# Attention and a gated convolution on one core: value products as half-row blocks between score couples

## The chip, the cores and the metric

The kernel runs on one core of one Trainium2 chip. The time is the device time of one launch in microseconds. Five runs of the kernel before gave 386.9, 384.28, 387.31, 382.95 and 384.23 us, a median of 384.28 us. The first of them is the one that was profiled: 386.9 us, of which the profile's span covers 385.1 us.

## The reference: what is computed

Eight batches, twelve heads, 448 positions, 64 numbers a head. First attention with a softmax that has an extra one in its sum; then, on the heads laid side by side (448 x 768), a projection to three parts, a circular convolution of the second part along the sequence by Fourier transform, the product of the three, and a last projection.

```
scores = (q @ k^T) / sqrt(64);  m = max over keys
attn   = exp(scores - m) / (sum exp(scores - m) + exp(-m) + 1e-9)
x      = heads of (attn @ v) side by side            # 8 x 448 x 768
x1, x2, x3 = split(x @ w_proj)                       # 768 -> 3 * 768
conv   = irfft(rfft(x2) * rfft(filter))              # along the 448 positions
out    = (x1 * conv * x3) @ w_out
```

The kernel leaves the maximum out, since exp(s - m) / (sum exp(s - m) + exp(-m)) is exp(s) / (sum exp(s) + 1).

## The kernel before

**Attention** works on pairs of heads, 48 of them (six a batch). The heads of a pair lie in the two halves of the 128 rows (64 numbers each). The 448 keys of a head are three tiles of 128 and a remainder of 64; the two remainders of a pair share one tile. So a pair has:

- a *score couple* for each of three key tiles (L770): two matmuls of 64 rows, one on each half of the array's rows, 448 columns each, into two adjacent PSUM banks; ACT takes the exponential of both at once (L777, 128 x 896 out of PSUM);
- one score matmul of the shared remainder tile (L772, all 128 rows) and its exponential (L783);
- the *rests* (L795): eight matmuls of 64 rows, alternating between the two halves, that multiply the remainder's exponentials with its values and start the sums of the value products;
- the *value products* (L803): 24 matmuls of all 128 rows and 65 columns (64 values and a column of ones, which gives the softmax sum); 12 for each head, into a bank for each head;
- `norm` on DVE (L816 to L818): one added, reciprocal, product, out of PSUM into `xb`; for some pairs a transpose on TensorE follows (L897), for the others a DMA transpose.

**The dense part** of a batch follows its attention: projection of the second part on folded data (L977), spectrum (L1004), product with the filter's spectrum on DVE, inverse (L1089), gates (L1050), last projection (L1162). It is worked on while the next batches' attention runs. The filter's own spectrum (L722, L725) is made once at the start, from `uw` (L715 on DVE), which waits for the DMA of the filter (L664) on POOL's queue.

**The order of all work** is made on the host before the program is written. Every step is a task with an engine, a cost, a wanted time (`ATT`, `SLOT`, `DENSE`, `PACE`, `FOLD`, `LOAD` and so on are the numbers that make the wanted times), what it needs and makes, and which buffers it takes and gives back. `Plan.run` walks through time and starts, on each engine, the first task in order of wanted time that is ready by the planner's account; the instructions are then written in that order. Each engine runs its own list strictly in that order. The eight PSUM banks are handed out by the planner (`spots`): score couples ("sc") and a pair's output ("op") take two adjacent banks, at most two of each at a time (`CAP`), everything else ("hy") one bank. `fillers` puts matmuls on an idle tile (L1248) into gaps of TensorE that the planner sees between 3 and 36 us of its clock.

Before the change, two score couples are usually one task (`both`), often with the previous pair's rests in the same task; the two heads' value products are a task each (`out_rest`).

Of the kernel before, what the change touches and what calls it, by code (L numbers as in the profile page):

```python
# [18 lines left out]
B, H, S, DH = 8, 12, 448, 64  # L19
D = H * DH  # L20
SP = 112
NST = S // SP
# [19 lines left out]
class Plan:  # L42
# [17 lines left out]
    FILL = (3.0, 36.0, 0.6)  # L60
    PAIRS = ("sc", "op")
    CAP = {"sc": 2, "op": 2, "hy": 5}
# [6 lines left out]
    def add(self, eng, cost, want, emit, need=(), make=(), take=(), give=(), dma=0.0, run=256, n=1, after=0.0, begun=(), late=0.0):  # L69
        self.tasks.append((want, len(self.tasks), eng, cost, emit, need, make, take, give, dma, after, run, n, begun, late))  # L70

    def run(self):
# [109 lines left out]

        while any(queue.values()):
            moved = False
            for e in queue:
                if free[e] > now + 1e-9:
                    continue
                for i, t in enumerate(queue[e][: self.WINDOW]):
                    if ready(t):
                        break  # L190
                else:
                    continue
                del queue[e][i]
# [10 lines left out]
                end = free[e] = now + t[3]  # L204
# [52 lines left out]
def kernel(  # L257
# [16 lines left out]
    EARLY1 = 3.56  # L274
    ATT = [0.74, 31.12, 90.92, 107.97, 154.61, 193.46, 231.91, 282.14]
    SLOT = [2.70, 6.66, 5.08, 5.83, 4.70, 0.35, 4.90, 4.50]
    DENSE = [45.16, 85.16, 124.09, 170.16, 216.54, 256.31, 315.08, 409.78]
    PACE = [2.27, 2.24, 1.74, 2.16, 1.15, 2.13, 0.54, 0.88]
    FOLD = [-0.15, 0.76, -31.49, -25.60, 10.65, 0.32, 9.43, 0.88]
    BPS = 1.26  # L280
    RE1 = 16.91
    WT = 2.03
    FT = 18.78
    HALVED = (2,)
    AHEAD = [0, 0, 46.94, 46.01, 34, 34, 34, 34]
    LEAD = [-8.41, 6.91, 5.34, 23.10]
    LOADS = ((1, 0), (1, 1), ("F", None), (0, None), (2, None), ("O", None))
    LOAD = [36.34, 20.13, 13.48, 39.00, 39.88, 46.37]
    STEP = 4.27
    FOLD0 = (39.83, 49.48, 37.97)  # L290
# [464 lines left out]

    T = {}

    def attention(i):
# [41 lines left out]
        def out_rest(u):  # L800
            for n in range(NST):
                for t in range(3):
                    nc.tensor.matmul(  # L803
                        out_bank(u)[:, n, :],
                        P["e"][1 + t][:, u * S + n * 128 : u * S + n * 128 + 128],
                        vn[b % 2][:, hp, 4 * u + t, :],
                        start=False,
                        stop=(n == NST - 1 and t == 2),
                    )
# [522 lines left out]
```

## Time and profile before

| | |
|---|---|
| median of five runs | 384.28 us (382.95 to 387.31) |
| the profiled run, and its span | 386.9 us, 385.1 us |
| TensorE matmuls | 3732, busy 369.9 us (96% of the span) |
| ACT, DVE, POOL busy | 265.7, 257.8, 113.4 us |
| TensorE busy in the first 40 us | 33.11 us |
| mean granted TensorE clock | 0.996 |
| moved by DMA | 58.73 MB, most of it in the first 125 us |

A group's line in the profile names the line of the kernel, the engine, the operation, what it writes and reads, the shape (rows\*columns of the weights, then the output) and how many there are; then the time that the engine was busy with them. A matmul's duration is its way through the array (some 190 ns for 65 columns); in a row of matmuls the next one starts long before, so the cost of one in a row is the distance between starts. In the timeline a line is a run of equal instructions: start, time to the end of the last one, and in brackets the idle time ahead of it and what ended it.

### The profile page before, as it was taken

The numbers are of one execution on the slowest core, as the hardware profiler recorded it, in microseconds if no ns is written. First come the engines' busy times: TensorE is split into PE (matmuls) and PEld (weight loads), VectorE is DVE, ScalarE is ACT, GpSimd is POOL, SyncE is SP. The second block draws the span as 40 slices with busy tenths as digits, with TensorE's granted clock in tenths as the row PEclk, the third lists the DMA queues.
The fourth block names the chain that finished last, engine by engine and source line by source line (L and its number), as shares of the span: only waits on it lengthen the run. The fifth ranks groups of instructions, "written<-read, shape, count | busy, mean of one in ns | idle before, by whom it ended". The sixth has DMA issues, their size and how long they took to land.

```text
span 385.1 us, 9634 instructions
## 1 busy us (share of the span) xinstructions
PE 369.9 (96%) x3732; PEld 236.6 (61%) x3732; DVE 257.8 (67%) x679; ACT 265.7 (69%) x460; POOL 113.4 (29%) x232
## 2 busy tenths in 40 slices
PE   8986999999999999999998999999999999999995
PEld 7655775566655666655764566556665567557653
DVE  6575849954888448975399748592489635971870
ACT  5876878555877869777776767678677776543543
POOL 5674934341761633543544421100000000000000
PEclk9998999999999999999999999999999999999999
DMA  9999999999999999999999943912220042103004
GB/s 208 257 216 249 220 226 206 136 171 203 221 208 183 195 278 208 214 192 258 242 239 150 232 116 92 213 43 103 62 31 2 2 124 69 43 0 124 0 2 163
DMA packets 134573, 58.73 MB, mean 153 GB/s; under 512 B 99389, under 2 KB 130944, under 8 KB 134528
## 3 DMA queue, kind: packets, MB, share of 16 engines
q1 hardware_dynamic: 97104, 48.35, 56.9%
q0 software_dynamic: 37184, 9.54, 27.5%
q8 instruction: 29, 0.48, 0.6%
q10 hardware_dynamic: 240, 0.23, 0.3%
q14 instruction: 16, 0.13, 0.1%
HBM read 43.86 MB, written 11.01 MB: 142 GB/s over the span
## 4 chain that ended last, share of the span: by engine, by line
PE 64%; DVE 17%; DMA 11%; issue 2%; POOL 2%; SPq 2%; ACT 1%; DVEq 0%; POOLq 0%
PE psum L1050 16%; PE psum L977 13%; PE psum L1162 13%; PE psum L803 7%; PE psum L770 6%; DVE t L1018 3%; DMA nat<-in_v_dram 3%; DMA filt<-in_moe_filter_fft_dram 3%; DMA kT<-nat 2%; DVE g L1065 2%; DMA nat<-in_q_dram 2%; DVE yh L1024 2%; PE psum L1004 2%; DVE xf L954 2%; PE psum L772 2%
## 5 line engine op out<-in xcount | busy, mean ns | idle before, releaser
L777 ACT ACTIVATE e<-psum 128x896 bf16<-128x896 f32 x144 | 125.6, 923 | 23.7 <-PE psum L770 23.1
L1050 PE MATMUL psum<-xT,wproj_bf 128*128 128x448 bf16 x576 | 121.2, 352 | 0.6 <-DVE g L1065 0.5
L1050 PEld LDWEIGHTS <-wproj_bf 128*128 128x128 bf16 x576 | 54.0, 97 | 44.8 <-issue 2.2
L977 PE MATMUL psum<-wproj_bf,xf 128*113 128x384 bf16 x384 | 69.6, 327 | 0.0
L977 PEld LDWEIGHTS <-xf 128*113 128x113 bf16 x384 | 49.4, 132 | 13.4 <-issue 1.9
L1162 PE MATMUL psum<-wout_bf,yT 128*128 128x384 bf16 x288 | 51.9, 326 | 0.2 <-DVE yT L1133 0.2
L1062 ACT CAST x<-psum 128x448 bf16<-128x448 f32 x48 | 25.7, 534 | 34.2 <-PE psum L1050 32.5
L803 PE MATMUL psum<-vn,e 128*128 128x65 bf16 x1152 | 45.2, 195 | 0.0
L1065 DVE TENSOR_TENSOR g<-x,psum 128x448 bf16<-128x448 bf16 x48 | 29.6, 616 | 19.4 <-PE psum L1050 18.1
L599 POOL CAST vn<-nat 128x192 bf16<-128x192 f32 x72 | 26.8, 399 | 51.9 <-DMA nat<-in_v_dram 38.0
L770 PE MATMUL psum<-qT,kT 64*128 64x448 bf16 x288 | 41.5, 358 | 0.0
L803 PEld LDWEIGHTS <-e 128*128 128x128 bf16 x1152 | 39.6, 98 | 2.8
L1174 ACT COPY osb<-psum 128x384 f32<-128x384 f32 x56 | 26.3, 485 | 20.3 <-PE psum L1162 19.8
L1162 PEld LDWEIGHTS <-yT 128*128 128x128 bf16 x288 | 27.3, 98 | 19.3 <-issue 1.6
L816 DVE TENSOR_SCALAR rec<-psum 128x8 f32<-128x8 f32 x48 | 7.8, 163 | 43.5 <-PE psum L803 42.7
L1018 DVE TENSOR_TENSOR t<-xs,hrs 113x768 bf16<-113x768 bf16 (+1 forms) x64 | 34.8, 581 | 2.5 <-ACT xs L1012 2.4
L818 DVE TENSOR_TENSOR xb<-psum,rec 128x512 bf16<-128x512 f32 x48 | 33.2, 691 | 1.7
L533 POOL DMA_DIRECT2D nat<-in_q_dram x28 | 24.9, 890 | 31.8 <-DMA qT<-nat 15.6
L989 DVE CAST x<-psum 113x384 bf16<-113x384 f32 x32 | 17.7, 553 | 24.4 <-PE psum L977 23.9
L1012 ACT CAST xs<-psum 113x384 bf16<-113x384 f32 (+1 forms) x64 | 28.0, 493 | 4.1 <-PE psum L1004 4.0
L991 ACT CAST x<-psum 113x384 bf16<-113x384 f32 x32 | 15.4, 481 | 19.7 <-PE psum L977 19.4
L1098 ACT CAST cr<-psum 128x452 bf16<-128x452 f32 x48 | 25.4, 551 | 5.0 <-PE psum L1089 4.8
(109 smaller groups left out, 447.5 us busy)
## 6 DMA issues: line engine op xcount, KB each, us to landing
nat<-in_k_dram SPq DMA_DIRECT2D x48, 192.0 KB, 5.2
nat<-in_v_dram SPq DMA_DIRECT2D x48, 192.0 KB, 5.3
out_dram<-osb SPq DMA_DIRECT2D x24, 384.0 KB, 2.7
nat<-in_q_dram POOLq DMA_DIRECT2D x20, 168.0 KB, 7.0
nat<-in_q_dram SPq DMA_DIRECT2D x11, 224.0 KB, 7.3
wproj_bf<-in_moe_w_proj_dram POOLq DMA_DIRECT2D x2, 1152.0 KB, 18.3
rests<-in_k_dram SPq DMA_DIRECT2D x8, 192.0 KB, 5.9
rests<-in_v_dram SPq DMA_DIRECT2D x8, 192.0 KB, 6.8
```

The costliest lines, as they stand in the source:

```text
L599: nc.gpsimd.tensor_copy(vn[b % 2][:, hp, 4 * u : 4 * u + 3, 0:DH], sv[:, u])
L770: nc.tensor.matmul(sc[:, u, 0:S], kT[b % 2][c, hp, t, :], qT[b % 2][c, hp, :])
L777: nc.scalar.activation(e[:, 0 : 2 * S].rearrange("p (u n) -> p u n", u=2), pair(("sc", ("S", i, t)))[:, :, 0:S], AF.Exp, scale=SCALE,)
L803: nc.tensor.matmul(out_bank(u)[:, n, :], P["e"][1 + t][:, u * S + n * 128 : u * S + n * 128 + 128], vn[b % 2][:, hp, 4 * u + t, :], start= ...
L818: nc.vector.tensor_tensor(W["xb", b][:, hp].rearrange("p n (u d) -> p u n d", u=2), op[:, :, :, 0:DH], rec[:].unsqueeze(3).to_broadcast([1 ...
L977: nc.tensor.matmul(pps[:FQ, :DCH], W["xf", b][:, pg, kt, 0:FQ], wproj_bf[:, kt, D + ch * DCH : D + (ch + 1) * DCH], start=(kt == 0), stop= ...
L1012: nc.scalar.copy(L["xs", par, ch][:K, pg % 2, :], L["Z", pg, ch][:K, :DCH])
L1018: nc.vector.tensor_tensor(t[:K], L["xs", par, ch][:K], h, op=ALU.mult)
L1050: nc.tensor.matmul(p[:, :S], wproj_bf[:, kt, 2 * part * D + dt * 128 : 2 * part * D + (dt + 1) * 128], xT()[:, kt, 0:S], start=(kt == 0), ...
L1065: nc.vector.tensor_tensor(g[:, dt, :], L["x1", dt], p[:, :S], op=ALU.mult)
L1162: nc.tensor.matmul(ops[:n, :DCH], y[:, dt, 0:n], wout_bf[:, dt, ch * DCH : (ch + 1) * DCH], start=(dt == 0), stop=(dt == NDT - 1),)
L1174: nc.scalar.copy(L["os", st][:n, ch * DCH : (ch + 1) * DCH], L["O", st, ch][:n, :DCH])
```

## The change

1. Every value product of 128 rows is split into two of 64 rows, one on each half of the array, so that the pair's products are 48 matmuls in place of 24. They come in two blocks of 24 (`values(0)`, `values(1)`): in the first, the lower half adds into head 0's bank and the upper half into head 1's; in the second the halves are swapped, so that the two matmuls that run beside each other never write the same bank. The second block's first matmul waits by a semaphore (`half_done`) until the first block's last one has written.
2. Score couples are single tasks; the rests and the first block are one task (`way`), the second block another. By their wanted times they follow each other as: couple 1 of pair i, rests and first block of pair i-1, couple 2, second block, couple 3.
3. Up to three score pairs may hold banks (`CAP`), in place of two.
4. The planner books a cost for each change on TensorE between tasks of half-row matmuls (`row`) and others (`TURN`); it lets TensorE wait up to `WAIT` for the next half-row task when it has just done one; it avoids putting a second block directly behind its first one (`apart`, `REACH`, `CLOSE`).
5. All wanted times are new numbers, so that the order of everything is new.

```diff
-    CAP = {"sc": 2, "op": 2, "hy": 5}
+    REACH = 2.43
+    TURN = 0.1
+    CLOSE = 0.12
+    WAIT = 0.31
+    CAP = {"sc": 3, "op": 2, "hy": 5}
...
-                    if ready(t):
+                    if near is not None and t[0] > queue[e][near][0] + self.REACH:
                         break
-                else:
+                    if not ready(t):
+                        if e == "PE" and t[15] and prev and prev[15]:
+                            later = soon(t)
+                            if later <= now + self.WAIT:
+                                heapq.heappush(events, max(later, now + 1e-6))
+                                hold = True
+                                break
+                        continue
+                    if prev is not None and t[16] in prev[6]:
+                        near = i if near is None else near
+                        continue
+                    at = i
+                    break
...
+                end = now + t[3]
+                if e == "PE":
+                    if close:
+                        end += self.CLOSE
+                    if t[15] != bool(prev and prev[15]):
+                        end += self.TURN
+                    prev = t
...
-    ATT = [0.74, 31.12, 90.92, 107.97, 154.61, 193.46, 231.91, 282.14]
+    ATT = [0.36, 42.32, 102.52, 113.36, 162.99, 193.84, 245.07, 281.01]
...
-        def out_rest(u):
+        def values(side):
+
             for n in range(NST):
                 for t in range(3):
-                    nc.tensor.matmul(
-                        out_bank(u)[:, n, :],
-                        P["e"][1 + t][:, u * S + n * 128 : u * S + n * 128 + 128],
-                        vn[b % 2][:, hp, 4 * u + t, :],
-                        start=False,
-                        stop=(n == NST - 1 and t == 2),
-                    )
+                    for low in range(2):
+                        u = low ^ side
+                        c = slice(64 * low, 64 * low + 64)
+                        now = nc.tensor.matmul(
+                            out_bank(u)[:, n, :],
+                            P["e"][1 + t][c, u * S + n * 128 : u * S + n * 128 + 128],
+                            vn[b % 2][c, hp, 4 * u + t, :],
+                            start=False, stop=(side == 1 and n == NST - 1 and t == 2),
+                        )
+                        if side and not n + t + low:
+                            behind(now, P["V"])
+            if not side:
+                P["V"] = mark(now)
...
+            if t:
+                add("PE", 0.195, tau(i) + 0.002 * t if i else w, lambda t=t: scores(t),
+                    need=[("kT", i), ("qT", i)] + ([("S", i, t - 1)] if t > 1 else [("S", i - 1, 3)] if i else []),
+                    make=[("S", i, t)], take=[("sc", ("S", i, t))], row=True)
...
+        def way():
+            out_rests()
+            values(0)
+
+        add("PE", 0.53, w + 0.003, way, need=[("e", i), ("ones", b % 2), "pads", ("v", i), ("vr", b)], make=[("V", i)],
+            take=[("op", i)], give=[("er", (i, 0))], row=True)
+        add("PE", 0.395, w + 0.005, lambda: values(1), need=[("V", i)], make=[("V", i, 0), ("V", i, 1)],
+            give=[("e", (i, t)) for t in range(1, 4)], row=True, apart=("V", i))
```

`mark` lets the matmul that it is given add one to `half_done`; `behind` lets a matmul wait until `half_done` has reached a count. `soon` gives the planner's time at which a half-row task that is not ready yet will be.

## The prediction

> **What bounds the kernel now.** I read the page's busy times first, then its slices and the chain of work that ended last.
>
> ```profile
> PE 369.9 (96%) x3732; PEld 236.6 (61%) x3732; DVE 257.8 (67%) x679; ACT 265.7 (69%) x460; POOL 113.4 (29%) x232
> ...
> PE   8986999999999999999998999999999999999995
> ...
> PE 64%; DVE 17%; DMA 11%; issue 2%; POOL 2%; SPq 2%; ACT 1%; DVEq 0%; POOLq 0%
> ```
>
> TensorE (PE) is busy 96% of the span, and the lower digits stand in the first four slices and the last. By stretches it is busy 33.11 of the first 40 us, 87.79 of the next 90, 98.73 of the next 100 and 96.85 of the next 97. So it idles 6.9 us in the first 40 and 3.6 us from there to 327 us, where attention ends. A change of its work counts nearly in full; what else can be won is mostly at the start.
>
> But busy hides how TensorE spends its time. For that I read the timeline of TensorE in the middle, taking distances between starts, not durations:
>
> ```profile
> 198.51 2.43 PE L1050 MATMUL psum<-xT,wproj_bf 128*128 128x448 bf16 x12
> 200.87 0.55 PE L770 MATMUL psum<-qT,kT 64*128 64x448 bf16 x4
> 201.26 0.28 PE L795 MATMUL psum<-vn,er 64*128 64x65 bf16 x8
> 201.48 0.93 PE L803 MATMUL psum<-vn,e 128*128 128x65 bf16 x24
> 202.24 0.35 PE L772 MATMUL psum<-qT,kT 128*128 128x448 bf16 x1
> ...
> 206.64 0.55 PE L770 MATMUL psum<-qT,kT 64*128 64x448 bf16 x4
> 207.12 0.38 PE L1089 MATMUL psum<-bt,yh 113*128 113x113 bf16 x4
> ...
> 340.21 2.43 PE L1050 MATMUL psum<-xT,wproj_bf 128*128 128x448 bf16 x12
> 342.48 2.11 PE L1162 MATMUL psum<-wout_bf,yT 128*128 128x384 bf16 x12
> ```
>
> Twelve gate matmuls take 2.27 us (340.21 to 342.48) when full rows follow, 2.36 (198.51 to 200.87) when half rows follow: 0.09 for the turn. Two score couples take 0.39 (200.87 to 201.26) before the rests, 0.48 (206.64 to 207.12) before full rows: 0.09 again. A visit to half rows costs about 0.19 us beside its work. A score couple takes 0.195. 24 full products take 0.76, 31.7 ns each; a half-row pair of the rests takes (0.22 - 0.09) / 4, with rounding 30 to 32.5 ns. So two half-row products beside each other cost about what one full one costs.
>
> **The change part by part.** The order of both programs' instructions can be compared without a run; counts below come from there.
>
> *Turns.* Before, TensorE visits half rows 79 times, now 70 times: 30 visits hold all of a pair (couple, rests, block, couple, block, couple), 13 a lone couple. 9 x 0.19 = **-1.7 us**. That is little: before, the products were full rows, and two couples with the rests shared a visit already.
>
> *Products.* 1152 full ones become 1152 pairs. At 30 ns -2.0 us, at 32.5 ns +0.9; I take 31 ns, **-0.8**. Bounds: the 65 columns still stream, 65 / 448 of the gate's 0.189 is 27 ns, -5.4; two halves that run one after the other at 31.7 ns each would be +36. The rests' row is nearest, since it is the same instruction in the same alternation, but it is only eight long and the blocks are 24.
>
> The rests lie 15 to 16 ns a matmul apart, two beside each other. The Trainium skill, "TensorE: Matmul & The Clock Gate", section "Wait — 56ns, not 53.3ns?", speaks against this: matmul starts never come closer than about 25 ns, however few the columns. By that rule 2304 halves would be at least 57.6 us in place of 36.5, and the kernel 21 us slower; the trace does not show that floor when the halves alternate.
>
> *The wait between the blocks.* The second block's first matmul waits for the first block's last write. That one is some 0.19 us long (the profile's mean for this shape), and TensorE starts 0.05 us after a release (DVE's `xb` ends at 205.12, the weight load that waits for it starts at 205.17): 0.24 us from its start. In 41 of 48 cases just a couple stands between, which brings the block there after 0.03 + 0.19 = 0.22; 0.02 to 0.03 is left, 1.2 us in all. Three times nothing stands between: 3 x 0.21. Four times more does. Together **+1.9**; queued behind it are only the couple and the dense work that follow.
>
> *Banks and ACT.* Three couples need 6 banks and the output 2, all eight. A couple's banks come free 0.36 (matmul) + 0.04 + 0.92 (exponential, 923 ns by the page) + 0.05 = 1.37 us after its start at the earliest. I walked both orders with the distances above and noted where a bank is written again sooner. Past the start-up, before: 0.1 us in all. Now third couples take the first one's banks after 1.25 us some eight times (0.12 each), and with some others 1.9 us are missing. Moreover batch 5's pairs stand close together: ACT's work, put against TensorE's order, piles up to 4.3 us there (2.2 at most before), and TensorE must wait for its banks, I take 2 us. Together **+3.9**. Bounds: nothing, where these waits take the place of others; 8 us, if each of 48 visits also holds up the dense result behind three exponentials (2.8 us in a row) by 0.1.
>
> *Start-up.* The timeline of DVE and TensorE around 32 us:
>
> ```profile
> 31.98 0.96 DVE L715 TENSOR_TENSOR uw<-filt 113x1536 bf16<-113x1536 bf16 x1 [2.85 <-DMA filt<-in_moe_filter_fft_dram]
> ...
> 34.04 0.43 PE L897 MATMUL psum<-ident_bf,xb 128*128 128x128 bf16 x4 [3.18 <-DVE xb L818]
> ...
> 36.55 1.40 PE L803 MATMUL psum<-vn,e 128*128 128x65 bf16 x24
> 37.79 0.35 PE L722 MATMUL psum<-uw,ft 113*113 113x384 bf16 x1
> ```
>
> DVE stands 2.85 us at the filter's sum with pair 4's `norm` queued behind; TensorE idles 3.18 us for that, and then runs at about half pace (24 products 1.24 us in place of 0.76). In the new DVE order pair 4's `norm` stands ahead of the filter's sum, and TensorE has pair 5's products to do meanwhile. The filter's DMA moves back behind one more pair of POOL casts (0.65 us), and the weights' first DMA behind it by about 1.9; that one was issued at 22.3 and landed 9 to 14 us later, well ahead of the first L977 (42.40). The filter's spectrum (37.79) could start near 31.98 + 0.7 + 0.96 = 33.7, 4.1 sooner; the k and q casts for the next transposes then set the pace. I take **-2.5** (bounds 0, if loads are late by as much, and -4.1). Nine fewer filler matmuls (81 to 72) only fill idle time.
>
> *Other waits.* The 3.6 us of idle time past 40 us are drawn anew; some fall into the new holds: **-0.8** (bounds -3.6 and +2). The end, 57 us of dense work with the same order, stays. DMA bytes and ACT's, DVE's and POOL's work stay; SP's list is the same in its first part.
>
> Sum: -1.7 - 0.8 + 1.9 + 3.9 - 2.5 - 0.8 = 0.0. Against its own run that is 386.9 us; the median of the runs shown is 2.6 below that one, so I forecast **384.3 us**. Within 1% is about what a measurement of this kernel can't tell from no change (the five runs span 1.1%).
>
> **The rivals.**
>
> *Faster.* Pairs at 30 ns (-2.0), the whole start-up gain (-4.1), holds of 1.5, others -1.5, turns and the wait as above: -1.7 - 2.0 + 1.9 + 1.5 - 4.1 - 1.5 = -5.9, **378.4 us**. For it: the 3.18 us stall has one visible cause and that is moved. Against: the loads behind it fill the DMA engines until 125 us.
>
> *Slower by issue.* Place: the 24-matmul blocks. A half-row pair is four instructions (two weight loads, two matmuls) where a full product was two; the longest such run before is sixteen instructions behind a long couple. If TensorE can't be fed four per 31 ns for a whole visit (124 instructions), the pair stretches. At 40 ns it costs 1152 x 9 = 10.4 us more than I took, **394.7 us**; it decides (over 1% slower) from about 34.5 ns a pair. For it: no row shows a longer run. Against: the rests and one late-released run keep the pace.
>
> *Slower by ACT.* Holds at their bound of 8 and a start-up gain of 0.5: 0.0 + 4.1 + 2.0 = +6.1, **390.4 us**. For it: ACT's pile of 4.3 us; against: ACT is busy only 69%, a pair's four exponentials need 3.3 us of some 6.
>
> *Does little of what it says:* three couples in one visit in only 30 of 48 pairs. That is in the forecast.
>
> **How the numbers follow.** Forecast's case 0.43, faster 0.29, slower by issue 0.13, slower by ACT 0.15. The range runs from the faster case to just beyond the ACT one, 378 to 391, and leaves out most of the issue case and the best of the faster one. Faster by over 1% 0.29, within 1% 0.43, slower by over 1% 0.28.
>
> **What would show it.** In the profile after: the distance between the starts of the blocks, 12 pairs in 0.37 us; 70 visits; second blocks 0.03 late behind a couple; the first filter spectrum matmul near 34 us and the first L977 line's successor near 40; TensorE's idle time past 40 us between 4 and 8 us, most of it ahead of score couples and in batch 5. Wrong it would be if blocks take over 0.42 us, or if loads in the first 125 us set the pace.

## The result, and the profile after

The changed kernel runs in 388.49 us (median; 384.71 to 391.62) where the kernel before, run beside it, takes 385.94 us (381.11 to 393.25). The ratio is 1.0081, with a 95% interval of 1.0067 to 1.0095: slower by 0.8%, or about 2.6 to 3 us. The ratio leaves out, for each kernel, the executions that took over 1.5% longer than its fastest. The profiled execution took 389.37 us; its span is 387.4 us, against 386.9 us and 385.1 us before. The last matmul starts 2.7 us later than before (383.0 against 380.3 us).

The forecast was no change. The time lies within the range and within 1%, but a difference is there. Of the forecast's six terms, the turns, the products and the wait between the blocks came out near their sizes and the banks somewhat smaller; the start-up and the other waits did not come out as said.

The page of the changed kernel, the lines that answer to those shown of before and two groups (after the bar: busy time, mean ns of one, idle time ahead and what ended it):

```profile
PE 370.6 (96%) x4875; PEld 236.3 (61%) x4875; DVE 260.3 (67%) x679; ACT 263.1 (68%) x460; POOL 110.6 (29%) x232
...
PE   8979899999999889999999999999999999999995
...
PE 65%; DMA 15%; DVE 10%; ACT 4%; issue 2%; POOL 1%; SPq 1%; POOLq 0%; ACTq 0%
...
L871 PE MATMUL psum<-vn,e 64*128 64x65 bf16 x2304 | 53.1, 191 | 2.2 <-issue 2.0
...
L834 PE MATMUL psum<-qT,kT 64*128 64x448 bf16 x288 | 51.6, 355 | 1.2 <-ACT e L841 0.4
```

TensorE has nearly the same busy time. In the chain of work that ended last, DMA has gone from 11% to 15% and DVE from 17% to 10%. Two things stand in the groups that before did not have: idle time ahead of score matmuls that an exponential ends, and 2.0 us of idle time in a value block with no releaser ("issue").

A pair's visit in the timeline (start, time to the end of the last one, shapes and count):

```profile
40.93 0.36 PE L834 MATMUL psum<-qT,kT 64*128 64x448 bf16 x2
41.13 0.28 PE L859 MATMUL psum<-vn,er 64*128 64x65 bf16 x8
41.25 0.54 PE L871 MATMUL psum<-vn,e 64*128 64x65 bf16 x24
41.64 0.35 PE L834 MATMUL psum<-qT,kT 64*128 64x448 bf16 x2
41.88 0.55 PE L871 MATMUL psum<-vn,e 64*128 64x65 bf16 x24
42.26 0.36 PE L834 MATMUL psum<-qT,kT 64*128 64x448 bf16 x2
```

Twelve half-row pairs take 0.38 to 0.39 us (41.25 to 41.64, 41.88 to 42.26); the second block starts 0.24 after the couple ahead of it (41.64 to 41.88) where a couple needs 0.19. So the blocks run as forecast. Where the time went is seen elsewhere: first at the start,

```profile
29.35 0.67 PE L871 MATMUL psum<-vn,e 64*128 64x65 bf16 x17 [2.00 <-issue]
...
34.19 0.33 PE L770 MATMUL psum<-uw,ft 113*113 113x384 bf16 x1
...
38.27 1.14 PE L1019 MATMUL psum<-wproj_bf,xf 128*113 128x384 bf16 x6
...
47.85 3.13 PE L1019 MATMUL psum<-wproj_bf,xf 128*113 128x384 bf16 x18 [1.50 <-DMA wproj_bf<-in_moe_w_proj_dram]
```

then in TensorE's waits past 40 us, first of the changed kernel, then of the kernel before (total, times, longest in us):

```profile
PE psum L836 <- DMA kT<-nat: 3.0, 2, 1.6
PE psum L1019 <- DMA wproj_bf<-in_moe_w_proj_dram: 1.5, 1, 1.5
PE psum L859 <- DVE xb L889: 0.5, 1, 0.5
PE psum L1092 <- DVE xb L889: 0.5, 1, 0.5
PE psum L834 <- ACT e L841: 0.4, 1, 0.4
```

```profile
PE psum L897 <- DVE xb L818: 2.0, 3, 1.0
PE psum L1050 <- DVE g L1065: 0.5, 1, 0.5
PE psum L1004 <- DVE x L989: 0.4, 1, 0.4
PE psum L772 <- DMA kT<-nat: 0.3, 1, 0.3
```

In these two executions the filter's spectrum starts at 34.19 (before: 37.79) and the first projection of the second part at 38.27 (42.40), 4.1 us sooner. (How much of this is the order's and how much the execution's is told below, under the start-up alone.) But the second piece of the projection's weights lands at 47.8 to 47.9 us in both, so the changed one waits for it; before asks for it at 48.05, 0.16 us after it has landed. The changed kernel also waits 3.0 us for transposed k at the first scores of batches 2 and 3 (at 127 and 143 us), where before waits 0.3.

A lag curve puts this in order: for each point of time of the kernel before, how much later (or sooner, negative) the changed kernel has done the same amount of matmul work, from the starts of all matmuls in the two traces. It compares one execution with one other, so the columns up to 51 us also hold what differs between executions. "Loads left out" and "and short exponentials" are pairs of runs told of below.

| us in the kernel before | 37 | 51 | 100 | 117 | 147 | 190 | 208 | 222 | 300 |
|---|---|---|---|---|---|---|---|---|---|
| after - before | -3.3 | -1.0 | -0.5 | -1.8 | +1.7 | +2.8 | +1.0 | +2.8 | +3.1 |
| same, loads left out in both | -1.4 | -1.0 | +0.5 | +0.4 | +1.3 | +1.4 | +0.7 | +3.3 | +2.9 |
| same, and short exponentials in both | +0.9 | +1.7 | +2.5 | +3.2 | +3.6 | +3.4 | +2.8 | +4.9 | +4.4 |

### The profile page after: what moved, and what is told of

Its sections match the earlier page's. It is cut to its first block, busy times and chain, and to the rows that moved or that the text cites. A ratio compares the mean times of both kernels' runs of the same rounds, so it can differ in the third digit from the quotient of the medians.

```text
span 387.4 us, 11896 instructions
## 1 busy us (share of the span) xinstructions
PE 370.6 (96%) x4875; PEld 236.3 (61%) x4875; DVE 260.3 (67%) x679; ACT 263.1 (68%) x460; POOL 110.6 (29%) x232
## 3 DMA queue, kind: packets, MB, share of 16 engines
q1 hardware_dynamic: 97104, 48.35, 58.7%
## 4 chain that ended last, share of the span: by engine, by line
PE 65%; DMA 15%; DVE 10%; ACT 4%; issue 2%; POOL 1%; SPq 1%; POOLq 0%; ACTq 0%
PE psum L1092 21%; PE psum L1019 14%; PE psum L1204 12%; DMA kT<-nat 5%; PE psum L871 5%; DMA nat<-in_k_dram 5%; PE psum L834 5%; DMA wproj_bf<-in_moe_w_proj_dram 3%; PE psum L1046 2%; DMA nat<-in_q_dram 2%; ACT e L841 2%; PE psum L836 2%; PE psum L1131 1%; DVE cv L1160 1%; DVE g L1107 1%
## 5 line engine op out<-in xcount | busy, mean ns | idle before, releaser
L871 PE MATMUL psum<-vn,e 64*128 64x65 bf16 x2304 | 53.1, 191 | 2.2 <-issue 2.0
L1204 PE MATMUL psum<-wout_bf,yT 128*128 128x384 bf16 x288 | 53.3, 327 | 0.5 <-DVE yT L1175 0.2
L834 PE MATMUL psum<-qT,kT 64*128 64x448 bf16 x288 | 51.6, 355 | 1.2 <-ACT e L841 0.4
L871 PEld LDWEIGHTS <-e 64*128 64x128 bf16 x2304 | 44.9, 94 | 9.0 <-issue 5.9
L1060 DVE TENSOR_TENSOR t<-xs,hrs 113x768 bf16<-113x768 bf16 (+1 forms) x64 | 35.8, 594 | 3.8 <-ACT xs L1054 3.7
L647 POOL CAST vn<-nat 128x192 bf16<-128x192 f32 x72 | 25.6, 387 | 41.8 <-DMA nat<-in_v_dram 36.6
L847 ACT ACTIVATE er<-psum 128x448 bf16<-128x448 f32 x48 | 27.1, 566 | 14.1 <-PE psum L836 14.1
```

Source lines behind the costliest of these rows:

```text
L834: nc.tensor.matmul(sc[:, u, 0:S], kT[b % 2][c, hp, t, :], qT[b % 2][c, hp, :])
L847: nc.scalar.activation(e[:, 0:S], bank(("hy", ("S", i, t)))[:, 0:S], AF.Exp, scale=SCALE)
L871: now = nc.tensor.matmul(out_bank(u)[:, n, :], P["e"][1 + t][c, u * S + n * 128 : u * S + n * 128 + 128], vn[b % 2][c, hp, 4 * u + t, :], ...
L1060: nc.vector.tensor_tensor(t[:K], L["xs", par, ch][:K], h, op=ALU.mult)
L1204: nc.tensor.matmul(ops[:n, :DCH], y[:, dt, 0:n], wout_bf[:, dt, ch * DCH : (ch + 1) * DCH], start=(dt == 0), stop=(dt == NDT - 1),)
```

## The experiments

Line numbers shift by one to twenty in some of these kernels; the operations' names tell which line is meant. All ratios are to the kernel before, run on the same chip beside them.

### Do the loads take the gain back? (both kernels without them)

The steps stay in the plan, so that the order is kept, but issue nothing: loads, casts and transposes of q, k and v for batches 2 to 7.

```diff
         def q_load(st, gs):
+            return
             nc.gpsimd.dma_start(
...
         def q_turn(st, gs):
+            return
             nc.sync.dma_start(
...
         def k_turn(hp):
+            return
             nc.sync.dma_start(
...
-                    lambda x=x, hp=hp, src=src: nc.sync.dma_start(src.rearrange("p (u c) -> p u c", u=2), rows(x, b, hp)),
+                    lambda: None,
...
```

> The changed kernel without the loads, transposes and casts of q, k and v for batches 2 to 7 (they compute on the data of batches 0 and 1); the order of TensorE is unchanged. Theory A (the gain at the start is given back where data arrives no sooner: the changed kernel's two long waits of TensorE for kT, 1.76 us at 127 and 1.55 us at 143): both waits go, 3 us or more sooner than the changed kernel, ratio to the kernel before 0.995 to 1.001. Theory B (holds for banks and ACT and the wait between blocks make the loss): the time stays, ratio 1.005 to 1.010. The wait for the second piece of the projection's weights at 47.9 us stays in both.

> The kernel before with the same loads, transposes and casts left out. Its TensorE waits only 0.3 us for kT past 50 us, so under both theories it stays within 0.4% of the kernel before (0.996 to 1.000). Theory A: the changed kernel without these loads (the run before this one) is as fast or faster than this one; theory B: it is still about 0.8% slower.

Measured: the changed kernel 381.98 us, 0.9917 (0.9884 to 0.9950); before 379.21 us, 0.9837 (0.9802 to 0.9872). By the ratios both gain about 6.3 us from their own time, and the distance stays 2.8 us. Both ratios lie below what either theory gave, for the gain of the kernel before was not expected; what decides is the distance, and it stays. So the loads cost both kernels the same, and "the loads take back the lead" is not the whole reason. In this pair the granted clock stays full until the end of the work in both traces. By the lag curve the lead at 37 us is just 1.4; the distance to the end then comes from about 100 to 147 us and, in one step of over 2 us, between 208 and 222 us, in batch 5.

### The start-up alone (before, with pair 4's norm ahead of the filter's sums)

```diff
-            add("DVE", 1.0, w - 1, lambda par=par: half(par), need=["filt"], make=[("uw", par)],
+            add("DVE", 1.0, w - 1, lambda par=par: half(par), need=["filt", ("xb", 4)], make=[("uw", par)],
```

> The kernel before with one edge more in its plan: the filter's sums on DVE wait for pair 4's norm, so that this norm stands ahead of them in DVE's order; TensorE's list changes only by fillers and by a few places. Theory A: TensorE's 3.18 us wait at 34 us goes and the first L977 line's matmul starts 2 to 4 us sooner, but the second piece of the weights still lands near 47.9 us and the end comes only 0 to 1.5 us sooner, ratio 0.996 to 1.000. The rival (the start sets the end): 2.5 to 4 us sooner, 0.990 to 0.994.

Measured: 386.21 us, 1.0025 (0.9989 to 1.0060): nothing gained, which is above what either side expected, though the interval reaches into theory A's range. In its timeline the projection stands for the weights:

```profile
46.55 1.73 PE L977 MATMUL psum<-wproj_bf,xf 128*113 128x384 bf16 x7 [2.51 <-DMA wproj_bf<-in_moe_w_proj_dram]
```

It leads the profiled execution of before by 4.3 us at 37 us and by nothing (0.2 late) at 51 us. That looks as if the edit had won 4.3 us and lost them again, but most of the 4.3 us are not the edit's. A later run shows this: the kernel before with half-row blocks (told of below), in which every engine's instructions up to this point stand in the same order as in before, but for the split products. There DVE meets no wait at the filter's sum, since the filter landed earlier, and the first projection starts at 38.40, 4.0 us sooner than in the profiled execution of before, without any edit of the start-up:

```profile
29.15 0.94 DVE L715 TENSOR_TENSOR uw<-filt 113x1536 bf16<-113x1536 bf16 x1
38.40 1.14 PE L997 MATMUL psum<-wproj_bf,xf 128*113 128x384 bf16 x6
46.33 1.83 PE L997 MATMUL psum<-wproj_bf,xf 128*113 128x384 bf16 x10 [1.88 <-DMA wproj_bf<-in_moe_w_proj_dram]
```

Stretches of the two executions, first before, then this one (from and to, length, TensorE's busy time and instructions, granted clock, DMA share, GB/s):

```profile
26.00:34.00 8.00, 3.87 (x57) 1.00 1.18 255
34.30:37.70 3.40, 3.40 (x47) 0.50 1.10 248
```

```profile
26.00:34.00 8.00, 6.43 (x158) 1.00 1.19 260
34.30:37.70 3.40, 3.40 (x31) 1.00 1.12 236
```

So the profiled execution of before lost time twice: in the stall of 3.18 us, and in the 3.4 us after it, in which the granted clock was 0.50. Both are missing in the other execution of the same order. The run with the edit has its first projection at 37.92, only 0.5 us sooner than that one.

What all these executions share is the weights' second piece. In this order the projection asks for it with its 19th matmul, which starts at 48.05 in before (no wait), at 46.33 in the run with half-row blocks (after 1.88 us) and at 46.55 in the run with the edit (after 2.51 us), each time within 0.2 us of the landing. The run with the edit pays once more for this wait, since the granted clock falls behind it:

```profile
47.40:50.80 3.40, 3.40 (x21) 0.50 1.14 220
```

So in the old order, too, what is won ahead of the weights' second piece ends at it.

### What the turns are worth (changed kernel with full-row products)

`values(side)` does one head's twelve products over all 128 rows, without mark and wait; all else stays, so that every block now is a visit's end and start: 149 visits in place of 70.

```diff
-                    for low in range(2):
-                        u = low ^ side
-                        c = slice(64 * low, 64 * low + 64)
-                        now = nc.tensor.matmul(
-                            out_bank(u)[:, n, :],
-                            P["e"][1 + t][c, u * S + n * 128 : u * S + n * 128 + 128],
-                            vn[b % 2][c, hp, 4 * u + t, :],
...
+                    u = side
+                    nc.tensor.matmul(
+                        out_bank(u)[:, n, :],
+                        P["e"][1 + t][:, u * S + n * 128 : u * S + n * 128 + 128],
+                        vn[b % 2][:, hp, 4 * u + t, :],
...
```

> The changed kernel's order with full-row products in the two blocks (12 of head 0, then 12 of head 1), without the wait between blocks. TensorE then changes between half and full rows 149 times in place of 70. If a visit costs 0.19 us and a half-row pair as much as a full product: +15.0 us for the visits, about -1.7 us for the wait between blocks, 1.038 to 1.045. If the half-row blocks are themselves dearer than full rows (issue): less than that, 1.02 or below.

Measured: 395.65 us, 1.0262 (1.0212 to 1.0313), 7.2 us over the changed kernel, between the two expectations. Past 40 us TensorE changes between half and full rows 249 times in place of 106; at 94 ns each that is 13.4 us. Against it, what visits take beyond their matmuls' pitch falls by 4.0 us (1.9 of it is the wait between the blocks), and what full-row matmuls take beyond theirs by 1.8: the waits for transposed k are not in this run's list of waits. 13.4 - 4.0 - 1.8 = 7.6. So here a part of the turns' price was hidden by waits that the changed kernel has and this run has not.

### What the half-row blocks cost by themselves (before, with blocks in place of its products)

The kernel before in its own order, `out_rest` replaced by the changed kernel's `values`, with `mark` and `behind`. In 47 of 48 pairs the second block follows directly.

```diff
-        def out_rest(u):
+        def out_rest(side):
             for n in range(NST):
                 for t in range(3):
-                    nc.tensor.matmul(
+                    for low in range(2):
+                        u = low ^ side
+                        c = slice(64 * low, 64 * low + 64)
+                        now = nc.tensor.matmul(
...
+                        if side and not n + t + low:
+                            behind(now, P["V"])
+            if not side:
+                P["V"] = mark(now)
```

> The kernel before, in its own order, with the two tasks of full-row products of each pair replaced by the two half-row blocks and their wait; nothing is left out. The visits to half rows stay 79. In 47 of 48 pairs nothing stands between the blocks. If a half-row pair costs what a full product costs (31.7 ns) and the direct wait about 0.21 us each, 47 x 0.21 = 9.9 us are added: ratio to before 1.026 (1.022 to 1.030). If the half-row pairs are cheaper by 0.7 ns or more (the 31 ns of the prediction), 0.8 less: 1.024. If the instruction stream cannot feed a longer chain (rests and two blocks in one visit) and pairs stretch to 34 ns, 2.6 more: 1.033 or above. If the wait is mostly hidden, under 1.015.

Measured: 393.9 us, 1.0195 (1.0131 to 1.0259), 5 to 10 us more. The ratio lies between the range expected for the full wait and the 1.015 under which the wait would have been mostly hidden; the trace tells which. The timeline of TensorE:

```profile
154.64 0.29 PE L809 MATMUL psum<-vn,er 64*128 64x65 bf16 x8
154.76 1.16 PE L820 MATMUL psum<-vn,e 64*128 64x65 bf16 x48
155.85 1.31 PE L1070 MATMUL psum<-xT,wproj_bf 128*128 128x448 bf16 x6
```

From 154.76 to 155.85 are 1.09 us: 24 pairs at 31.6 ns (0.76), the turn (0.09), and 0.22 between the blocks. Over all blocks past 40 us, from start to start inside a block: half-row pairs 31.6 ns here and 31.5 ns in the changed kernel; full products 32.0 ns before. The direct wait is 0.22 us (0.220 to 0.241) in each of 41 pairs past 40 us, 9.2 us in all. In the changed kernel, with a couple between, the wait is 0.043 us over the couple (39 pairs, 1.68 us, and one direct of 0.22). So the issue rival falls, here with 48 half-row products in a row, and the alternation of couples and blocks saves what the blocks' own wait would cost. (The profiled execution of this run is only 4.8 us longer than that of before, since it has no stall and no halved clock at the start.)

### Batch 5's knot and the weights' piece (four runs)

Where batch 5 begins, TensorE waits twice in the changed kernel:

```profile
218.48 0.36 PE L834 MATMUL psum<-qT,kT 64*128 64x448 bf16 x2 [0.44 <-ACT e L841]
219.36 0.30 PE L859 MATMUL psum<-vn,er 64*128 64x65 bf16 x8 [0.51 <-DVE xb L889]
```

The first run halves ACT's work there, the second lets batch 0's second projection read the columns of the weights that landed first, the third does both; the fourth has the edit of `need` above and the second edit on the kernel before.

```diff
-                    e[:, 0 : 2 * S].rearrange("p (u n) -> p u n", u=2), pair(("sc", ("S", i, t)))[:, :, 0:S], AF.Exp,
+                    e[:, 0 : 2 * S].rearrange("p (u n) -> p u n", u=2)[:, :, w], pair(("sc", ("S", i, t)))[:, :, w], AF.Exp,
```

with `w = slice(0, S // 2 if b == 5 else S)`, and

```diff
-                    wproj_bf[:, kt, D + ch * DCH : D + (ch + 1) * DCH],
+                    wproj_bf[:, kt, D + (ch if b else 1) * DCH : D + ((ch if b else 1) + 1) * DCH],
```

> The changed kernel, in which the exponentials of batch 5's score couples (counted from 0) take only the first half of each head's columns; the rest of the tile keeps what an earlier pair left there. Order and everything else are unchanged. Knot theory (three pairs of batch 5 stand so close that TensorE waits for ACT's exponentials, 1.3 us at 218 us, and the changed kernel falls back by 2 us there): 1.3 to 2.5 us sooner than the changed kernel, ratio to the kernel before 1.002 to 1.005. Rival (the loss is spread over all pairs, by the wait between blocks and issue): unchanged, 1.007 to 1.009.

> The changed kernel, in which batch 0's second projection reads the weights' piece that landed first (columns 384 to 767 of the part) for both halves, so that it doesn't wait for the piece that lands at 47.8 us. If the start's lead is lost at this wait alone: the 1.5 us wait goes and stays gone, ratio 1.002 to 1.005. If the lead would be lost later anyway (kT, batch 5): 1.007 to 1.009.

> The two edits of the runs before this one together. If both waits are causes of their own, they add up: 3 to 4 us sooner than the changed kernel, 0.998 to 1.001 of the kernel before. If one only makes room for the other: as the better of the two.

> The kernel before with pair 4's norm ahead of the filter's sums, as in the run before on this, and with batch 0's second projection reading the weights' piece that landed first for both halves. With the norm alone TensorE waited 2.5 us for the second piece and the end did not move (1.0025). If that wait is what ate the start's lead: 2 to 3 us sooner than the kernel before, 0.992 to 0.996. If the lead is lost later anyway: 0.999 to 1.003.

Measured, in this order: 1.0036 (1.0000 to 1.0072), 1.0026 (0.9987 to 1.0065), 1.0013 (0.9980 to 1.0047), 0.9995 (0.9956 to 1.0033). By these ratios the edits take 1.7 and 2.1 us off the changed kernel's 1.0081, the two together 2.6, not clearly more than one; the fourth run stands 1.2 us below the 1.0025 of the run with the norm alone, less than the two intervals can tell apart. The first ratio lies where the knot theory put it, but its trace does not bear the theory out. It leads the changed kernel's profiled execution by 2.8 us at 48 us, long before its edit acts, because its stop in the value block at 29 us is shorter (1.1 us for 2.0), no halved clock follows, and the weights' second piece lands at 45.0 us; from 208 to 222 us, where the knot is, it wins nothing. In the trace of the second run the wait for the piece is gone and 1.6 us are won between 45 and 48 us and kept. That is as expected, but the first run gains 1.4 us at the same place without the edit. The trace of the fourth run shows what becomes of a lead that gets past the second piece. It is 3.5 us ahead of before's profiled execution at 51 us, then TensorE waits for the third piece of the weights, for which before does not wait (it lands at 55.3 us there, and the gates start at 56.52), and by 60 us the run is 1.2 us behind:

```profile
56.18 2.42 PE L1050 MATMUL psum<-xT,wproj_bf 128*128 128x448 bf16 x6 [2.99 <-DMA wproj_bf<-in_moe_w_proj_dram]
```

Halving the exponentials does not undo the knot. In the first run's timeline the wait for ACT is gone, and the rests wait 1.13 us for DVE instead of 0.51:

```profile
214.40 0.75 PE L834 MATMUL psum<-qT,kT 64*128 64x448 bf16 x4
216.29 0.30 PE L860 MATMUL psum<-vn,er 64*128 64x65 bf16 x8 [1.13 <-DVE xb L890]
```

```profile
214.70 0.50 DVE L992 TENSOR_TENSOR w<-xT 128x678 bf16<-128x678 bf16 x1
215.12 0.15 DVE L888 TENSOR_SCALAR rec<-psum 128x8 f32<-128x8 f32 x1
215.30 0.20 DVE L889 RECIPROCAL rec<-rec 128x8 f32<-128x8 f32 x1
215.54 0.69 DVE L890 TENSOR_TENSOR xb<-psum,rec 128x512 bf16<-128x512 f32 x1
```

The previous pair's blocks end near 214.6; its `norm` stands behind a fold (`w`) on DVE until 215.12 and ends at 216.23, and only then are the two output banks free for the next rests. Three pairs follow each other here with little dense work between them, so that the wait for ACT hid one for the output banks. At this place the loss is not made by ACT's length alone.

### All of ACT's waits (short exponentials in batches 1 to 7, no loads)

The loads are left out as above, and the couples' exponentials cover half the columns for all batches but the first (`if b` in place of `if b == 5`).

> The changed kernel without the loads, transposes and casts of q, k and v for batches 2 to 7, and with the exponentials of the score couples of batches 1 to 7 over the first half of each head's columns only (about 0.55 us in place of 0.94); the order of all instructions is that of the changed kernel. Without loads alone the changed kernel ran 0.9917, before 0.9837, 2.8 us apart. Theory: most of that distance is TensorE waiting for banks and results behind ACT's exponentials (holds of some 2.8 us by the trace, 1 us of them in batch 5); then this falls to 0.983 to 0.986, and stands 0 to 1 us from the same cut of before. Rival: the distance is the fixed price of the blocks (the wait between blocks, their pitch) and DVE's norm; then it stays at 0.989 or above, 2 us or more over the same cut of before.

> The kernel before with the same work left out as in the run beside it: loads, transposes and casts of q, k and v for batches 2 to 7, and half the columns of the couples' exponentials of batches 1 to 7. Before hardly waits for ACT (about 1.5 us in all visits past 40 us, some of it for banks): both theories expect 0.980 to 0.984.

Measured: changed 381.26 us, 0.9869 (0.9824 to 0.9914); before 379.02 us, 0.9812 (0.9761 to 0.9863): still 2.2 us apart. By the times alone that decides little, since each interval is 1.7 to 2 us wide to each side. The lag curve speaks against the theory that most of the distance is TensorE waiting behind ACT; it gives ACT less than a third: from 51 us to 300 us the lag grows by 3.9 us without loads and by 2.7 us when ACT is short as well. Before gains nothing from short exponentials past its start: its two traces stay 1.4 to 1.5 us apart from 40 us to the end. The knot is there as in the run before, now as one wait for the output banks:

```profile
PE psum L861 <- DVE xb L891: 1.0, 1, 1.0
```

### Two score pairs in place of three

```diff
-    CAP = {"sc": 3, "op": 2, "hy": 5}
+    CAP = {"sc": 2, "op": 2, "hy": 5}
```

> The changed kernel planned with at most two score pairs holding banks in place of three; everything else is the same, nothing is left out, and the order is planned anew by the same numbers. It makes 75 visits in place of 70: 5 x 0.19 = 1.0 us more for turns. If third couples cost more by holding up dense results than they save, the holds fall by 1 to 2.8 us and the batch 5 knot by up to 1.5: ratio to before 1.000 to 1.006, below the changed kernel's 1.008. If the three pairs pay, 1.010 or above.

Measured: 396.52 us, 1.0253 (1.0183 to 1.0323). That looks like 6.6 us for the third pair, but the trace does not say so: up to 190 us this run is ahead of the changed kernel by 0.8 us, and by 208 us it is 4.3 us behind. Of these 5.1 us, 3.6 are a single wait of TensorE at 194 us, and the granted clock is 0.50 in the 3.4 us behind it (an estimate of 1.7 us, half of these, makes up the rest):

```profile
194.50:197.90 3.40, 3.40 (x33) 0.50 1.03 282
```

The first two of the next three runs have the same wait, of 4.6 and 1.6 us. What the third pair is worth stays open.

### Moving the waits for transposed k away (three runs)

```diff
-    ATT = [0.36, 42.32, 102.52, 113.36, 162.99, 193.84, 245.07, 281.01]
+    ATT = [0.36, 42.32, 105.02, 116.36, 162.99, 193.84, 245.07, 281.01]
-    AHEAD = [0, 0, 42.12, 61.23, 34, 34, 34, 34]
+    AHEAD = [0, 0, 44.62, 64.23, 34, 34, 34, 34]
```

The second run shifts both numbers by 1.5; the third leaves `ATT` and has 45.12 and 64.23 in `AHEAD`.

> The changed kernel with only the wanted times of attention of batch 2 moved 2.5 us and of batch 3 3.0 us later, their loads' wanted times kept; nothing left out, 70 visits as before. The changed kernel's trace has 3.3 us of TensorE waits for transposed k at 127 and 143 us, at the first scores of batches 2 and 3. If TensorE merely asked too early there, with other work at hand, the waits go and the ratio to before falls by 1.5 to 3 us: 1.000 to 1.004. Rival: the loads pace the whole stretch, and the wait comes back at the next load or as dense work that runs out: 1.006 to 1.010.

> As the run beside it, with shifts of 1.5 us for both batches; 71 visits. If the waits are a matter of the wanted times, about half of them goes: 1.002 to 1.006. Rival as there: 1.006 to 1.010.

> The changed kernel with only the wanted times of the loads of batches 2 and 3 moved 3 us earlier; nothing left out, 69 visits. If the transposed k of batches 2 and 3 comes late because its chain of loads, casts and transposes starts late, the waits at 127 and 143 us go: 1.000 to 1.004. If the transfers themselves fill the time until then, starting them earlier pushes back others (the projection's weights land at 47.8 us) and nothing is gained: 1.006 to 1.012.

Measured: 1.0297 (1.0244 to 1.0349), 1.0238 (1.0186 to 1.0290), 1.0175 (1.0119 to 1.0230). All are outside both expectations. In none of the three does TensorE still wait for the DMA that transposes k, and yet each loses more elsewhere: the second has a wait of 4.1 us for `xb` at 127 us, the third waits of 1.7 and 2.0 us for the filter's sum and the weights. TensorE's two longest waits in the first run, and DVE's around the second one:

```profile
PE psum L834 <- DVE x L1031: 4.6, 1, 4.6
PE psum L939 <- DVE xb L889: 2.3, 1, 2.3
```

```profile
186.57 0.56 DVE L1031 CAST x<-psum 113x384 bf16<-113x384 f32 x1 [1.73 <-PE psum L1019]
193.53 0.32 DVE L988 COPY xT<-xT 128x6 bf16<-128x6 bf16 x1 [6.40 <-DMA xT<-xb]
193.88 0.51 DVE L991 TENSOR_TENSOR u<-xT 128x678 bf16<-128x678 bf16 x1
194.31 0.51 DVE L991 TENSOR_TENSOR w<-xT 128x678 bf16<-128x678 bf16 x1
194.73 0.55 DVE L1031 CAST x<-psum 113x384 bf16<-113x384 f32 x1
195.20 1.32 DVE L1060 TENSOR_TENSOR t<-xs,hrs 113x768 bf16<-113x768 bf16 x2
```

Before the wait of 4.6 us DVE stands 6.4 us for a DMA transpose of `xb`, with a projection's copy queued behind it; the score couple at 195.34 needs that projection's bank, and TensorE stops. In the run with two score pairs the same chain costs 3.6 us (DVE 5.5 us for the transpose). The changed kernel itself has such waits of DVE, 8.4 us in four, and the kernel before no group of them that reaches 2.9 us; they stay hidden in the changed kernel since dense work is at hand then. So the rival is right in substance, though not in size: late transfers come back in the next place. They can do so as late as 190 us, since the DMA engines are busy far longer than the 125 us of the text ahead of the result. The page of before has nines to about 221 us, and 26.0 of the 58.7 MB move in the first 125 us:

```profile
DMA  9999999999999999999999943912220042103004
```

It is shown that the wait for transposed k can be moved; it is not shown that any order gets rid of the time. No run of the whole work was clearly faster than the kernel before.

## Why the prediction was wrong

| term | forecast, us | measured, us | from |
|---|---|---|---|
| turns | -1.7 | -1.7 | 158 changes before, 140 now, 94 ns each |
| products | -0.8 | -0.5 | 31.97 to 31.53 ns, 1152 pairs |
| wait between the blocks | +1.9 | +1.9 | 39 x 0.043 + 0.22, past 40 us; 2.4 with the start (41 and 3 direct) |
| banks and ACT | +3.9 | +2.9 | other excess in visits past 40 us: 4.4 now, 1.55 before |
| start-up | -2.5 | about -1.0, of two executions | lag at 51 us, the wait for the weights included |
| other waits | -0.8 | about +1.4 | what full-row matmuls take past 40 us beyond their pitch: 8.7 now, 7.3 before |
| sum | 0.0 | +3.0 | measured +2.55 by medians, +2.7 at the last matmul of the profiled executions |

The step that failed is the start-up: a gain of 2.5 us that no run shows. Without it the forecast's own terms sum to +2.5, which is about what was measured; that this is so close is luck, for the banks came out 1.0 too high and the other waits 2.2 too low.

*Turns and wait*: right in mechanism. The count and the 94 ns are as forecast; the wait behind a couple is 0.04 us on average (up to 0.06), a little over the 0.02 to 0.03 of the forecast. The turns' row is the count times the price and was not measured by itself.

*Products*: right in mechanism, the size a little off, because full products cost 32.0 ns over all 41 pairs and not the 31.7 of one row, and half-row pairs 31.5 and not 31. The floor of about 25 ns between matmul starts that the Trainium skill states ("TensorE: Matmul & The Clock Gate", "Wait — 56ns, not 53.3ns?") is not seen where the two halves alternate: inside the blocks the 2304 matmuls lie 15.8 ns apart on average.

*Banks and ACT*: the size is too high and the cause half wrong. Waits ahead of couples and a knot in batch 5 are there, some 1.3 us of it in the knot (0.62 and 0.68 late at 218.5 and 219.4), but ACT's length is not what makes most of them: halving ACT's time takes away 1.2 of 3.9 us in the lag. What else is needed, DVE's `norm` for the two output banks, was not in the walk that gave the 3.9.

*Start-up*: this step failed, in two places. First, the gain was read from one execution. The stall of 3.18 us and the half pace after it (granted clock 0.50 for 3.4 us) belong to the profiled execution of before and not to its order: the same order ran without both in the run with half-row blocks, and moving pair 4's norm by itself gained nothing (1.0025). The forecast then applied its sum, with this gain in it, to the median of five runs, which lies 2.6 us below that execution. Of 74 executions of before that were timed beside the experiments, the 24 with a mean granted clock of 0.997 or more took 384.8 us (median) and the other 50 387.3 us; how many of these have the stall at the filter is not on record, since only one was profiled. Second, that the weights land "well ahead of the first L977" was true of the first piece; the second piece was not looked at. It lands at 47.8 to 47.9 us in both profiled executions, and the projection's 19th matmul starts with it (48.05 before, 47.85 after 1.5 us of waiting now), so that what is won ahead of it ends there. With that wait taken out, too, the lead ended at the third piece, at 56 us (the run of before with both edits of the start). The 2.0 us stop in a block at 29.35 us, with DVE's next `norm` behind it and a granted clock of 0.50 from 29.0 to 32.4 us, is not in the prediction either. At 51 us the new order leads by 1.0 us in the pair without loads, in which neither trace has a halved clock; the changed kernel's profiled execution, which has one, is 0.5 us behind the run with half-row blocks, which has none. So the new start is worth about 1 us at most, as far as these traces show.

*Other waits*: wrong sign. The forecast took the 3.6 us of old waits as a pool from which something could be won. They were, and the new order has others in their place: TensorE stands 3.0 us for transposed k. What the prediction named as its own undoing, "loads in the first 125 us set the pace", applies to the start and to these waits, but as the runs without loads show, not to the whole distance, since loads cost both kernels the same 6.3 us. The bound of +2 holds the term. The idle time past 40 us lies between 4 and 8 us as said (7.4), but most of it ahead of the weights and the transposed k and not ahead of couples.

The rivals: *issue* falls (31.5 ns). *ACT* is the smaller part of the waits in visits, by the lag curve. *Faster* falls since its 4.1 us at the start are mostly those of one execution, and what is won there ends at the weights.

What stays open: how the 2.9 us in visits divide, beyond ACT and the knot; and whether the two edits of the knot and the weights' piece together give more than one of them. Their intervals are 0.3 to 0.4% wide to each side, and the profiled execution of the two has a wait of 3.5 us at 124 us, with a granted clock of 0.50 for 6.8 us there, that neither of the others has. The rows of the table come from one execution of each kernel and hold what differs between executions.

## What to carry to other kernels

A stall in one profiled execution need not belong to the order: before a gain is booked on it, profile the same kernel again and see whether it is there, and do not take the gain off a median that may not contain it. A stall that a reordering does remove is worth only what the next transfer due lets through: look up the landing time of every later piece that the released engine will ask for. Two 64-row matmuls of 65 columns side by side cost here what one 128-row matmul costs (31.5 and 32.0 ns), so the split is worth the turns it saves and little more, and an accumulating second block needs a score couple's time of other work ahead of it to hide its wait (0.04 us in place of 0.22). In a densely planned order a changed due time takes one wait away and brings another, so a single planner number says little about the part of the change that it stands for.

## What was not expected of the hardware

TensorE stops in a value block with no releaser ahead of the same matmul of the program, the 480th, in eight of the ten kernels with the changed start and half-row blocks: 2.0 us in the changed kernel, 0.5 with loads left out, 1.1 and 1.2 with the short batch 5 and the weights' columns, 1.7, 1.5, 0.8 and 0.2 in the four re-planned runs. In two it does not: with the short batch 5 and the weights' columns together, and without loads and with short exponentials. The instruction queue moves 0.62 MB in 38 packets where the kernel before moves 0.48 MB in 29; but the kernel before with half-row blocks also moves 38 packets and has no such stop. That the instructions come late while the loads fill the DMA engines would fit; it was not tested.

Behind some of TensorE's waits the granted clock falls to 0.50 for 3.4 us: behind those of 3.18 us in before, 2.51 us in the run with the start-up's edit, 2.99 us in the run that waits for the third piece and 3.62 us in the run with two score pairs; in the changed kernel during the stop of 2.0 us. Behind the 4.56 us of the first re-planned run it lasts 6.8 us. Behind others it does not fall (1.88 us in the run with half-row blocks, 1.5 us at 47.85 in the changed kernel). A wait that brings it costs TensorE up to 1.7 us more, by estimate, than the wait itself; what decides whether it comes is not shown here.

A direct wait of TensorE on its own previous matmul's write costs 0.22 us beyond the pitch, in 41 places, all between 0.220 and 0.241 us.
